# Moving the first scores of a second batch behind the half-steps of an MLP, with later attention work shifted by one to three places

## The chip, the cores and the metric

The kernel runs on one core of a Trainium2 chip. A time is device microseconds (us) of one launch, as the median of three runs. Beside the runs there is one execution taken by the hardware profiler; its span goes from the first to the last instruction of the core.

Five engines work side by side, each through its own queue in order: TensorE (PE: matrix products, with the weight loads shown as PEld), VectorE (DVE), ScalarE (ACT), GpSimd (POOL), and SyncE (SP), which here only issues DMAs. TensorE writes into banks of PSUM, and the other engines read them from there.

## The reference

Windowed attention over 8 batches of 8 heads, 576 tokens, head size 64, and then a two-layer MLP over all 4608 tokens, 512 wide, with 2048 hidden units:

```python
scores = scale * np.matmul(q, k.transpose(0, 1, 3, 2))
mask_plain = (rel >= 0) & (rel < window)                      # window = 32, heads 0-3
mask_dil = (rel >= 0) & (rel < window * dilation) & (rel % dilation == 0)   # dilation = 4, heads 4-7
...
attn = np.exp(scores - max) ; attn = attn / (sum + 1e-09)
x = matmul(attn, v)  ->  (4608, 512)
h = x @ w_in
g = np.where(pos, h, np.where(neg, 0.0, (h + beta) ** 2 / (4.0 * beta)))    # beta = 1
return (g @ w_out).astype(np.float32)
```

The weights are given as 64-bit floats, q and k are 8 times larger than drawn, and the output is 32-bit.

## The kernel before

**The MLP.** The tokens are cut into 9 tiles of 512 (`t`), the hidden units into 16 blocks of 128 (`f`). A *step* `s` is one pair (t, f); there are 144. `layer1(t, f)` makes 12 products of 512 columns into one of two PSUM banks `h` (4 chunks of the model width, three terms each, because a 32-bit factor is split into a high and a low part). Then comes the activation of the step, in this order: `y` on VectorE (L418), a square on ScalarE (L421), `h` on VectorE (L423), a rounded copy `gh` on ScalarE (L424), the remainder `gl` on VectorE (L427). `layer2` makes 12 products into the banks `acc0` to `acc3`, two steps later (`lag = 2`): the loop body of step s is `layer1(s)`, `run(2s)`, `layer2(s-2)`, `run(2s+1)`. The bank `h` of step s is free for step s+2 after its `gl`.

**The slots.** `run(u)` executes what `place(u, ...)` put into slot u. An even slot 2s stands behind `layer1(s)`, an odd slot 2s+1 behind `layer2(s-2)`. So pieces of attention stand between the layers, one piece at a place. In steps 0 and 1 there is no `layer2` yet, so slots 0 and 1, and slots 2 and 3, stand behind the second half of a `layer1`: its first half (chunks 0 and 1) of both steps is issued before the loop.

**The attention.** The heads of batch 0 (0 to 7) are computed before the loop. Those of batch 1 (8 to 15) run in pairs in the slots: `scores_pair(n, 0, 4)` and `scores_pair(n, 4, 6)` are 8 and 4 products (two rows of the trace each), and each product is followed by one VectorE instruction (L182) that adds the mask, writes the scores into `c` and keeps the row minimum (of the negated scores). `after_pair(n)` is the softmax of both heads, and it issues the next load of q and k, on the DMA queue of SyncE. For the heads 8, 9, 10, 12 and 14 `whole(n)` does a subtraction on GpSimd (L297), one exponential on ScalarE (L298) and one sum on VectorE (L299); for the others six exponentials on ScalarE do all three. Then a reciprocal (L291), and a product with it on GpSimd (L292). `transpose_pe(n)` makes six transposes on TensorE into two banks and copies them out (L334: four tiles on ScalarE, two on VectorE). `values_native(n)` is 24 products of the pair (rows L366) into two banks, which `store_x` copies out as `xh` on ScalarE (L350) and `xl` on VectorE (L351). Pairs 10 to 14, all transposes from head 8 on and all values take their banks from the tag `att`, of which there are two, in turn; pair 8's scores alone take `acc0` to `acc3`. Batches 2 to 7 (`scores_split`) follow from slot 27 on, on the same two `att` banks.

**The weights.** `weights(f, ...)` turns a 64-bit block into a high and a low 32-bit part: ScalarE (L116, L122, L132), VectorE (L124, L127) and GpSimd (L133). In steps 1 to 15 the loop prepares block s of `w_out` and s+3 of `w_in`, queued behind the activation of step s-2 (`behind`).

**Who sets the order.** On TensorE and on SyncE's DMA queue the order is that of the program (`manual_schedule`). On the other three engines a planner orders the instructions by when it expects their inputs, and among those that are ready by their place in the program less an offset (`tc.high_priority(offset=...)`): 100 for the row minima and the copies of transposes, 60 for the activation and for `store_x`, none for the weights. Nothing reorders the queues at run time.

**Before the change** pair 8's scores stand before the loop, after the first halves of steps 0 and 1 (L591, L592); `after_pair(8)` is queued behind the last stores of batch 0. At step 2, where TensorE waits for the first activation, 14 products of a constant (`spin(14, acc[0])`, L615) into bank `acc0` stand ahead of `layer1`; they compute nothing that is used.

Of the kernel before, what the change touches and what calls it, by code (L numbers as in the profile page):

```python
# [30 lines left out]
B, H, S, D = 8, 8, 576, 64  # L31
DM, DF = 512, 2048
WIN, DIL = 32, 4
QT, NQ = 96, 6
# [11 lines left out]
def body(ctx, tc, q, k, q2, k2, v, mask, eye, w_in, w_out, out):  # L46
# [105 lines left out]
    def bank(n):  # L152

        if n > H:
            return "att", 2
        turn[0] += 1
        return banks[(turn[0] - 1) % len(banks)]
# [3 lines left out]
    def spin(times, bank):  # L161

        half = half_t.broadcast_to([128, 128])
        for _ in range(times):
            PE.matmul(out=bank[:, :128], lhsT=half, rhs=half, start=True, stop=True)  # L165
# [27 lines left out]
    def scores_pair(n, t0, t1):  # L193

        pair = (n, n + 1)
        plain = n % H < H // 2
        svs = []
        for m in pair:
            if t0 == 0:
                begin(m)  # L200
            tag, bufs = bank(n)
            sp = ps.tile([128, 512], F32, tag=tag, name=f"s{m}_{t0}", bufs=bufs)
            svs.append(sp[:QT, : (t1 - t0) * 128].rearrange("p (t j) -> p t j", j=128))
            if m == 0 and t0 == 0:
                spin(11, sp)
        for t in range(t0, t1):
            for m, sv in zip(pair, svs):
                PE.matmul(
                    out=sv[:, t - t0],
                    lhsT=heads[m]["qs"][:, t * QT : (t + 1) * QT],  # L210
                    rhs=heads[m]["ks"][:, t * QT : t * QT + 128],
                    start=True,
                    stop=True,
                )
        with tc.high_priority(offset=100 if n >= H else 0):
            for t in range(t0, t1):
                for m, sv in zip(pair, svs):
                    which = (0 if t == 0 else 2) if plain else t % 3
                    reduce(m, t, (sv[:, t - t0], msk[:, which]))
# [102 lines left out]
    def pt_of(n):  # L322
        return first_pts[n] if n < len(first_pts) else pts[n % 2]

    def transpose_pe(n):
        pt, c = pt_of(n), heads[n]["c"]
        for t0, t1 in ((0, 4), (4, NQ)):
            tag, bufs = ("att", 2) if n == 0 or n >= H else bank(n)
            tp = ps.tile([128, 512], F32, tag=tag, name=f"t{n}_{t0}", bufs=bufs)
            for t in range(t0, t1):  # L330
                PE.transpose(tp[:, QT * (t - t0) : QT * (t - t0 + 1)], c[:, t], ident)  # L331
            copy = nc.scalar.copy if t0 == 0 else nc.vector.tensor_copy
            with tc.high_priority(offset=100):
                copy(out=pt[:, t0:t1], in_=tp[:, : QT * (t1 - t0)].rearrange("p (t j) -> p t j", j=QT))  # L334
# [62 lines left out]
    def layer1(t, f, cs=range(NC), bank=("h", 2)):  # L397
        xh, xl = xtile(t)
        if cs[0] == 0 and (t, f) not in hps:
            hps[t, f] = ps.tile([128, TOK], F32, tag=bank[0], name=f"h{t}_{f}", bufs=bank[1])  # L400
        hp = hps[t, f]
        terms = [(w, x, c) for c in cs for w, x in ((0, xh), (1, xh), (0, xl))]
        for i, (w, x, c) in enumerate(terms):
            PE.matmul(  # L404
                out=hp,
                lhsT=wi[f][:, w, 128 * c : 128 * c + 128],
                rhs=x[:, c],
                start=c == 0 and i == 0,
                stop=c == NC - 1 and i == len(terms) - 1,
            )  # L410
        if cs[-1] < NC - 1:
            return
        del hps[t, f]
        y = pool.tile([128, TOK], F32, tag="y", name=f"y{t}_{f}")
        gh = pool.tile([128, TOK], F32R, tag="gh", name=f"gh{t}_{f}", bufs=2)
        gl = pool.tile([128, TOK], F32R, tag="gl", name=f"gl{t}_{f}", bufs=2)
        with tc.high_priority(offset=60):
            nc.vector.tensor_scalar(  # L418
                out=y, in0=hp, scalar1=-1.0, scalar2=1.0, op0=ALU.max, op1=ALU.min
            )  # L420
            nc.scalar.activation(out=y, in_=y, func=AF.Square, bias=half_t, scale=0.5)  # L421

            activated = nc.vector.tensor_tensor(out=hp, in0=hp, in1=y, op=ALU.max)  # L423
            copied = nc.scalar.copy(out=gh, in_=hp)  # L424
            if t == 0:
                last["g", f] = copied, activated
            nc.vector.tensor_tensor(out=gl, in0=hp, in1=gh.bitcast(F32), op=ALU.subtract)  # L427
        gs[t, f] = gh, gl

    acc = {}  # L430
# [28 lines left out]
    def place(u, *ops):  # L459
        slots.setdefault(u, []).extend(ops)  # L460

    def after_pair(n):
        softmax(n)
        softmax(n + 1)
        if n + 4 < native:
            load_pair(n + 4)
        elif n + 4 == native:
            load(native)
        else:
            split(native)  # L470
            load(native + 1)
# [8 lines left out]
    def values_native(n):  # L480
        values(n)
        if n + 2 < native:
            load_values(n + 2)

    for n, at in ((8, (5, 6, 7)), (10, (1, 2, 8, 9, 10)), (12, (11, 12, 16, 17, 18)), (14, (19, 20, 24, 25, 26))):
        if n > H:
            place(at[0], lambda n=n: scores_pair(n, 0, 4))
            place(at[1], lambda n=n: (scores_pair(n, 4, NQ), after_pair(n)))
        place(at[-3], lambda n=n: transpose_pe(n))
        place(at[-2], lambda n=n: transpose_pe(n + 1))  # L490
        place(at[-1], lambda n=n: values_native(n))
    for n in range(native, nhead, 2):
        u = 27 + 4 * (n - native)
# [47 lines left out]
    def early_values(n):  # L541
        with tc.high_priority(offset=150):
            values(n)
# [14 lines left out]
    with tc.manual_schedule(engines={mybir.EngineType.PE, mybir.EngineType.SP}):  # L558
        pair(0)
        pair(2)  # L560
        pair(4)
        pair(6)
        hps[0, 0] = ps.tile([128, TOK], F32, tag="h", name="h0_0", bufs=2)
        early_transposes(0)
        load_values(8)
        fetch(1, w_out, "wo")
        fetch(4, w_in, "wi")
        load_pair(10)
        fetch(2, w_out, "wo")
        fetch(5, w_in, "wi")  # L570
        fetch(3, w_out, "wo")
        for f in range(6, 9):
            fetch(f, w_in, "wi")
            fetch(f - 2, w_out, "wo")
        early_values(0)
        early_transposes(2)
        early_values(2)
        first = marks()
        spin(10, hps[0, 0])
        early_transposes(4)  # L580
        spin(3, hps[0, 0])
        early_transposes(6)
        behind(first, ("wi", 0), ("wi", 1))
        early_values(4)
        second = marks()
        layer1(0, 0, range(2))
        early_values(6)
        third = marks()
        behind(second, ("wi", 2))
        layer1(0, 1, range(2))  # L590
        scores_pair(H, 0, 4)  # L591
        scores_pair(H, 4, NQ)  # L592
        for f in range(9, 14):
            fetch(f, w_in, "wi")
            fetch(f - 2, w_out, "wo")
        with tc.issue_after(third[0].ins), tc.issue_after(third[1].ins):
            after_pair(H)
        behind(third, ("wo", 0), ("wi", 3))
        l2 = 0
        steps = [(t, f) for t in range(NT) for f in range(NF)]  # L600
        lag = 2
        for s in range(len(steps) + lag):
            if s == 3:
                for f, src, name in ((12, w_out, "wo"), (13, w_out, "wo"), (14, w_in, "wi")):
                    fetch(f, src, name)
                for f, src, name in ((14, w_out, "wo"), (15, w_in, "wi"), (15, w_out, "wo")):
                    fetch(f, src, name)
            if 0 < s < NF:
                todo = [("wo", s)]
                if s + 3 < NF:  # L610
                    todo.append(("wi", s + 3))
                behind(last["g", max(s - 2, 0)], *todo)
            if s == 2:
                acc[0] = ps.tile([128, DM], F32, tag="acc0", name="acc0_0")
                spin(14, acc[0])  # L615
            if s < 2:
                layer1(*steps[s], range(2, NC))
            elif s < len(steps):
                layer1(*steps[s])
            run(2 * s)  # L620
            while l2 <= s - lag and l2 < len(steps):
                layer2(*steps[l2])
                l2 += 1
            run(2 * s + 1)
        assert not slots
# [63 lines left out]
```

## Time and profile before

| | us |
|---|---|
| Median of 3 runs (929.95 to 930.34) | 930.11 |
| Span of the profiled execution | 928.6 |
| Time outside the span (difference) | 1.5 |
| TensorE busy in the span | 907.2 |
| VectorE busy | 684.2 |
| ScalarE busy | 487.0 |
| GpSimd busy | 239.6 |

In these views a row is a start, a duration, an engine and a source line, and "out<-in". An idle time in brackets is the time in which the engine stood just before the row, with the instruction whose result it then waited for. TensorE's busy time is that of pipelined products and is no measure of how well it is used; where it stands still is read from the brackets and from the view of waits.

### The profile page before, as it was taken

Reading aid. Unit: us, or ns where it says so; the run is one execution under the profiler, and the core shown is the slowest. Engines: PE = TensorE matmul, PEld = TensorE weight load, DVE = VectorE, ACT = ScalarE, POOL = GpSimd, SP = SyncE. Lnnn points to the kernel's source line nnn. Section 1 sums busy time; section 2 is a strip of 40 time slices with the busy share of each in tenths; the row PEclk is TensorE's granted clock in tenths of the full one; section 3 lists DMA queues with packets and bytes.
Section 4 is the critical chain, followed back from the end, with each engine's and each line's share of the span. In section 5 each row is a group of like instructions: output and inputs, shape, how many; then the busy total and the mean of one; then the engine's idle time right before and its main releaser. Section 6 shows DMA issues by size and latency. Waiting matters only on the chain.

```text
span 928.6 us, 14426 instructions
## 1 busy us (share of the span) xinstructions
PE 907.2 (98%) x4886; PEld 743.4 (80%) x4886; DVE 684.2 (74%) x1982; ACT 487.0 (52%) x1336; POOL 239.6 (26%) x155
## 2 busy tenths in 40 slices
PE   7889989999999999999999999999999999999998
PEld 6667778888888888888888888888888888888886
DVE  6898877878888888878887888888878643334333
ACT  5778865655555555555555555555555322222222
POOL 4566452222222222222222222222222000000000
PEclk9999999999999999999999999999999999999999
DMA  9971001322232223222322123222321010001001
GB/s 351 408 294 54 1 27 46 113 70 70 70 115 69 54 58 102 70 70 70 105 82 68 59 58 115 70 70 71 115 70 43 1 46 1 1 1 46 0 1 46
DMA packets 31018, 73.87 MB, mean 80 GB/s; under 512 B 3520, under 2 KB 3808, under 8 KB 30944
## 3 DMA queue, kind: packets, MB, share of 16 engines
q1 hardware_dynamic: 30944, 72.94, 24.1%
q8 instruction: 39, 0.64, 0.3%
q14 instruction: 35, 0.29, 0.1%
HBM read 63.49 MB, written 9.44 MB: 79 GB/s over the span
## 4 chain that ended last, share of the span: by engine, by line
PE 89%; DVE 5%; ACT 3%; DMA 1%; issue 1%; POOL 1%; DVEq 0%; POOLq 0%; ACTq 0%
PE acc L440 41%; PE h L404 39%; PE s L231 4%; PE o L366 3%; DVE c L182 1%; ACT c L256 1%; DVE wo_raw L124 1%; DMA wi_raw<-w_in 1%; DVE wi_m L127 1%; DVE wo_m L127 1%; PE s L165 1%; PE t L331 0%; POOL c L292 0%; DVE c L299 0%; DVE xl L351 0%
## 5 line engine op out<-in xcount | busy, mean ns | idle before, releaser
L440 PE MATMUL acc<-wo,gh 128*128 128x512 f32 x1152 | 384.0, 395 | 0.0
L404 PE MATMUL h<-xh,wi 128*128 128x512 f32 x1152 | 357.2, 391 | 2.2 <-DVE gl L427 2.2
L440 PEld LDWEIGHTS acc<-wo,gh 128*128 128x128 f32 x1152 | 217.2, 189 | 47.6
L404 PEld LDWEIGHTS h<-xh,wi 128*128 128x128 f32 x1152 | 209.0, 188 | 40.7 <-DVE gl L427 2.6
L440 PE MATMUL acc<-wo,gl 128*128 128x512 f32 x576 | 225.7, 392 | 0.0
L404 PE MATMUL h<-xl,wi 128*128 128x512 f32 x576 | 224.3, 389 | 0.0
L144 POOL TENSOR_TENSOR kk<-kr,kk 128x608 fp32r<-128x608 f32 x48 | 94.8, 1975 | 412.8 <-ACT kk L140 412.8
L256 ACT ACTIVATE c<-c 96x128 f32<-96x128 f32 x330 | 128.9, 391 | 120.6 <-DVE c L182 120.6
L421 ACT ACTIVATE y<-y,consts 128x512 f32<-128x512 f32 x144 | 104.2, 723 | 121.1 <-DVE y L418 121.0
L424 ACT CAST gh<-h 128x512 fp32r<-128x512 f32 x144 | 84.4, 586 | 126.6 <-PE acc L440 124.3
L418 DVE TENSOR_SCALAR y<-h 128x512 f32<-128x512 f32 x144 | 99.2, 689 | 57.7 <-PE h L404 57.4
L423 DVE TENSOR_TENSOR h<-h,y 128x512 f32<-128x512 f32 x144 | 100.6, 699 | 49.7 <-ACT y L421 48.3
L404 PEld LDWEIGHTS h<-xl,wi 128*128 128x128 f32 x576 | 108.2, 188 | 23.1
L427 DVE TENSOR_TENSOR gl<-h,gh 128x512 fp32r<-128x512 f32 x144 | 98.5, 684 | 36.6 <-ACT gh L424 36.6
L440 PEld LDWEIGHTS acc<-wo,gl 128*128 128x128 f32 x576 | 108.6, 189 | 19.8
L307 DVE STREAM_TRANSPOSE pt<-c 32x192 f32<-32x192 f32 x288 | 106.1, 368 | 6.6 <-POOL c L292 3.2
L250 DVE TENSOR_TENSOR c<-s,msk 96x256 f32<-96x256 f32 (+1 forms) x168 | 61.4, 377 | 36.6 <-PE s L231 35.6
L292 POOL TENSOR_TENSOR c<-c 96x768 f32<-96x768 f32 x56 | 82.9, 1482 | 16.4 <-DVE c L291 14.1
L182 DVE CUSTOM_DVE_ANT_0 c<-s,c 96x128 f32<-96x128 f32 x288 | 70.5, 280 | 1.0
L256 ACT ACTIVATION_READ_ACCUMULATOR c<-c 96x1 f32 x330 | 61.8, 187 | 0.0
L350 ACT CAST xh<-o 128x288 fp32r<-128x288 f32 (+8 forms) x112 | 38.5, 383 | 38.9 <-PE o L366 23.8
L231 PEld LDWEIGHTS s<-kk,qs 128*96 128x96 f32 x288 | 46.4, 161 | 15.5
(57 smaller groups left out, 644.9 us busy)
## 6 DMA issues: line engine op xcount, KB each, us to landing
kr<-k_in SPq DMA_DIRECT2D x56, 304.0 KB, 3.4
qr<-q_in SPq DMA_DIRECT2D x56, 288.0 KB, 2.8
vt<-v_in SPq DMA_DIRECT2D x32, 384.0 KB, 4.0
out<-out SPq DMA_DIRECT2D x36, 256.0 KB, 3.1
wi_raw<-w_in SPq DMA_DIRECT2D x16, 512.0 KB, 9.7
wo_raw<-w_in SPq DMA_DIRECT2D x16, 512.0 KB, 9.7
msk<-mask_in SPq DMA_DIRECT2D x1, 144.0 KB, 3.7
ident<-eye_in SPq DMA_DIRECT2D x1, 36.0 KB, 4.4
```

The lines of the kernel that those rows point to most:

```text
L144: nc.gpsimd.tensor_tensor(out=kk[:, 1], in0=hd["kr"], in1=kk[:, 0].bitcast(F32), op=ALU.subtract)
L231: PE.matmul(out=sv[:, t - t0], lhsT=hd["qs"][:, t * QT : (t + 1) * QT], rhs=hd["ks"][:, :, t * QT : t * QT + 128], start=True, stop=True,)
L256: last["act"] = nc.scalar.activation(out=c[:, t], in_=c[:, t], func=AF.Exp, bias=st[:, 0, t : t + 1], scale=-1.0, accum_out=st[:, 1, t : t ...
L292: nc.gpsimd.tensor_tensor(out=c, in0=c, in1=spread(st[:, 2]), op=ALU.mult)
L307: nc.vector.transpose(out=pt[r : r + 32, :, 32 * g : 32 * g + 32], in_=c[32 * g : 32 * g + 32, :, r : r + 32],)
L404: PE.matmul(out=hp, lhsT=wi[f][:, w, 128 * c : 128 * c + 128], rhs=x[:, c], start=c == 0 and i == 0, stop=c == NC - 1 and i == len(terms) - 1,
L418: nc.vector.tensor_scalar(out=y, in0=hp, scalar1=-1.0, scalar2=1.0, op0=ALU.max, op1=ALU.min)
L421: nc.scalar.activation(out=y, in_=y, func=AF.Square, bias=half_t, scale=0.5)
L423: activated = nc.vector.tensor_tensor(out=hp, in0=hp, in1=y, op=ALU.max)
L424: copied = nc.scalar.copy(out=gh, in_=hp)
L427: nc.vector.tensor_tensor(out=gl, in0=hp, in1=gh.bitcast(F32), op=ALU.subtract)
L440: PE.matmul(out=acc[m], lhsT=g[:, r], rhs=wo[f][:, w], start=f == 0 and i == 0, stop=f == NF - 1 and i == len(terms) - 1,)
```

## The change

Four things change. Pair 8's scores go into slots 1 and 3, behind the second halves of steps 0 and 1, and lose the rule that queued their softmax behind the stores of batch 0. All later places of batch 1 move: pair 10's scores from slots 1, 2 to 4, 5; its transposes from 8, 9 to 10, 11; its values from 10 to 12; pair 12 by one place; pair 14's scores by one, its transposes from 24, 25 to 25, 26 with head 15 ahead of head 14, its values from 26 to 29. Pair 8's transposes move from 5, 6 to 7, 8, its values from 7 to 9. The activation gets an offset of 120, and so precedes the row minima and all other work with a priority, in every step. `spin(14)` becomes `spin(6)`.

```diff
-        with tc.high_priority(offset=60):
+        with tc.high_priority(offset=120):
             nc.vector.tensor_scalar(
                 out=y, in0=hp, scalar1=-1.0, scalar2=1.0, op0=ALU.max, op1=ALU.min
             )
...
-    for n, at in ((8, (5, 6, 7)), (10, (1, 2, 8, 9, 10)), (12, (11, 12, 16, 17, 18)), (14, (19, 20, 24, 25, 26))):
-        if n > H:
-            place(at[0], lambda n=n: scores_pair(n, 0, 4))
-            place(at[1], lambda n=n: (scores_pair(n, 4, NQ), after_pair(n)))
-        place(at[-3], lambda n=n: transpose_pe(n))
-        place(at[-2], lambda n=n: transpose_pe(n + 1))
+    for n, at in ((8, (1, 3, 7, 8, 9)), (10, (4, 5, 10, 11, 12)), (12, (12, 13, 17, 18, 19)), (14, (20, 21, 25, 26, 29))):
+        place(at[0], lambda n=n: scores_pair(n, 0, 4))
+        place(at[1], lambda n=n: (scores_pair(n, 4, NQ), after_pair(n)))
+        turns = (n, n + 1) if n < 14 else (n + 1, n)
+        for u, m in zip(at[-3:-1], turns):
+            place(u, lambda m=m: transpose_pe(m))
         place(at[-1], lambda n=n: values_native(n))
...
-        scores_pair(H, 0, 4)
-        scores_pair(H, 4, NQ)
         for f in range(9, 14):
             fetch(f, w_in, "wi")
             fetch(f - 2, w_out, "wo")
-        with tc.issue_after(third[0].ins), tc.issue_after(third[1].ins):
-            after_pair(H)
         behind(third, ("wo", 0), ("wi", 3))
...
-                spin(14, acc[0])
+                spin(6, acc[0])
```

After the change slot 12 holds two pieces, the values of pair 10 and then the first scores of pair 12, and slot 29 the values of pair 14 and then the last scores of head 16.

## The prediction

> **What bounds the kernel now.** I read the page first, then the waits, then TensorE's timeline around the change. The page's forty slices show the engine that sets the end, and the one behind it:
>
> ```profile
> PE   7889989999999999999999999999999999999998
> DVE  6898877878888888878887888888878643334333
> ```
>
> TensorE is full from the fourth slice on. Every microsecond in which it stands still early is therefore paid at the end one for one, if nothing later has slack to take it up. The waits of TensorE, over the whole span, say how much there is:
>
> ```profile
> PE s L208 <- DVE c L182: 3.8, 7, 1.2
> PE t L331 <- POOL c L292: 2.8, 2, 2.6
> PE h L404 <- DVE gl L427: 2.2, 2, 1.2
> PE o L366 <- DVE pt L334: 1.8, 1, 1.8
> PE t L331 <- DVE xl L351: 1.4, 1, 1.4
> ```
>
> No wait is listed for the steady part (batches 2 to 7). All that the change can win or lose lies before about 150 us, in these holes:
>
> ```profile
> 38.22 1.55 PE L208 MATMUL s<-kr,qr 64*96 64x128 f32 x24
> 39.70 0.73 PE L404 MATMUL h<-xh,wi 128*128 128x512 f32 x2
> ...
> 41.27 1.12 PE L208 MATMUL s<-kr,qr 64*96 64x128 f32 x16
> 42.32 0.74 PE L404 MATMUL h<-xh,wi 128*128 128x512 f32 x2
> ...
> 45.18 0.46 PE L208 MATMUL s<-kr,qr 64*96 64x128 f32 x2 [1.19 <-DVE c L182]
> 46.03 0.67 PE L208 MATMUL s<-kr,qr 64*96 64x128 f32 x6 [0.39 <-DVE c L182]
> 46.63 3.39 PE L165 MATMUL acc<-consts 128*128 128x128 f32 x28
> 51.06 0.73 PE L404 MATMUL h<-xh,wi 128*128 128x512 f32 x2 [1.04 <-DVE gl L427]
> ...
> 58.48 0.73 PE L404 MATMUL h<-xh,wi 128*128 128x512 f32 x2 [1.16 <-DVE gl L427]
> ...
> 66.57 1.37 PE L366 MATMUL o<-pt,vt 128*64 128x96 f32 x24 [1.80 <-DVE pt L334]
> ...
> 72.92 0.36 PE L331 MATMUL t<-ident,c 96*128 96x96 f32 x2 [1.42 <-DVE xl L351]
> ```
>
> From the end of step 1's half to step 2 at 51.06, TensorE does little of use: 1.19 + 0.39 + 1.04 idle and 3.39 of constant products, 6.0 us; step 3 waits 1.16 more. These 7.2 us have one cause, the late first activation:
>
> ```profile
> 38.84 0.85 DVE L124 TENSOR_SCALAR wo_raw<-wo_raw 128x512 uint32<-128x512 uint32 x1
> ...
> 43.61 0.68 DVE L418 TENSOR_SCALAR y<-h 128x512 f32<-128x512 f32 x1
> ...
> 50.33 0.68 DVE L427 TENSOR_TENSOR gl<-h,gh 128x512 fp32r<-128x512 f32 x1
> ```
>
> Step 0's layer1 ends near 41.3, but `gl` only at 51.0: the 24 row minima of both pairs and softmax sums stand ahead of it. VectorE is not idle meanwhile; it is the second bound, as the windows show (columns: PE, PEld, DVE, ACT, POOL busy, then clock):
>
> ```profile
> 44.00:52.00 8.00, 5.39 (x40) 4.71 (x41) 8.00 (x34) 7.53 (x19) 4.05 (x3) 1.00 1.02 405
> 60.00:70.00 10.00, 8.20 (x58) 6.60 (x57) 9.62 (x11) 5.57 (x11) 7.44 (x6) 1.00 0.55 188
> ```
>
> The last large hole is pair 14's first transpose:
>
> ```profile
> 114.37 0.68 PE L208 MATMUL s<-kr,qr 64*96 64x128 f32 x8
> ...
> 128.71 0.71 PE L331 MATMUL t<-ident,c 96*128 96x96 f32 x6 [2.56 <-POOL c L292]
> ```
> ```profile
> 129.43 4.37 PE acc L440 x12
> ...
> 141.44 2.73 PE h L404 x12
> ```
> ```profile
> 126.00:136.00 10.00, 7.44 (x33) 5.96 (x33) 6.66 (x12) 4.37 (x9) 3.48 (x3) 0.83 0.01 2
> ```
>
> (The last rows are of the chain of waits and of the windows.) The hole costs twice: 2.56 idle, and after it a layer takes 4.37 where others take 2.73 (1.64 more): the granted clock of these ten microseconds is 0.83, against 1.00 in the windows above.
>
> **The change part by part.**
>
> *Start (steps 0 to 3).* The products moved are the same, 24 rows here and 24 there, so their TensorE time cancels. After the change TensorE goes at 38.22 straight into step 0's half (39.70 to 41.27 before: 1.57), 8 products of pair 8 (41.27 to 42.32: 1.05), step 1's half (about 1.57) and 4 products (0.68): 43.1. Then the 6 constant products wait for bank `acc0`, the bank of head 8's last two tiles, so for the third-last of pair 8's row minima. VectorE's work from 38.84 on is then: two weight blocks (to 41.16), 12 minima (2.54, two rows each), and y, h and gl of step 0 and y of step 1 (0.68 each: 2.7):
>
> ```profile
> 41.16 2.54 DVE c L182 x24
> ```
>
> That ends at 46.4 if all of it lies ahead of that minimum. Six constant products take 6/14 of 3.39: 1.45. So step 2's layer1 starts at about 47.9, and from 43.1 the hole is 4.8 where it was 7.2: **+2.4**. Pair 10's scores now come after step 2 and step 0's layer2 and have a layer between their halves; their wait of 1.19 + 0.39 is inside the 7.2. Best case: only one `y` ahead of that minimum, and `gl` in time (44.4 and 1.45: step 2 at 45.9, hole 2.8), +4.4. Worst: `gl` ends where it ends now, at 51.0, hole 7.9, -0.7.
>
> *Steps 3 to 5: 1.80 at pair 8's values and 1.42 at head 10's transposes.* Both are VectorE running late: the copy `pt` and the store `xl` sit in an in-order queue behind weight work that stretches to several times its length whenever GpSimd runs:
>
> ```profile
> 53.41 2.82 DVE L124 TENSOR_SCALAR wo_raw<-wo_raw 128x512 uint32<-128x512 uint32 x1
> ...
> 68.73 0.41 DVE L124 TENSOR_SCALAR wo_raw<-wo_raw 128x512 uint32<-128x512 uint32 x1
> ```
>
> The change removes no VectorE work, and keeps the distances (values one layer after head 9's transposes, head 10's transposes one layer after the values). I let the 1.42 stand and take half of the 1.80: **+0.9**. Ends: both go, +3.2; or a VectorE that is full to the brim gives back the whole lead of the start, -2.9.
>
> *Pair 14.* The chain from the end of its last scores (115.05) to head 14's normalised `c` (just before 128.71) is 13.6 us. Four layers of 2.73 cover 10.9 now. After the change the distance from slot 21 to slot 26 is five layers and head 15's transposes (0.5): 14.15. Head 15 goes first; its `c` is ready by 122.9, almost six us earlier:
>
> ```profile
> 121.44 1.47 POOL L292 TENSOR_TENSOR c<-c 96x768 f32<-96x768 f32 x1 [1.37 <-DVE c L291]
> ```
>
>  The cover is 0.5, and a `y` ahead of the minima (0.68) can eat it, so I leave a hole of 0.4: **+3.8** of 4.2. Ends: +4.2, and +2.4 (a hole of 1.80, which at 66.57 did not lower the clock). Pair 12 moves as a whole by one place: nothing.
>
> *Two slots with two pieces.* New waits arise in slots 12 and 29. Values take both `att` banks, and the scores right behind them need those banks again, after `store_x` has emptied them. Now a layer lies between:
>
> ```profile
> 79.28 1.21 PE L366 MATMUL o<-pt,vt 128*64 128x96 f32 x24
> ...
> 83.41 1.12 PE L208 MATMUL s<-kr,qr 64*96 64x128 f32 x16
> ```
> ```profile
> 72.48 0.29 DVE L351 TENSOR_TENSOR xl<-o,xh 128x128 fp32r<-128x128 f32 x1
> ...
> 82.88 0.28 DVE L351 TENSOR_TENSOR xl<-o,xh 128x128 fp32r<-128x128 f32 x1
> ```
> ```profile
> 137.00 1.21 PE L366 MATMUL o<-pt,vt 128*64 128x96 f32 x24
> ```
> ```profile
> 139.81 0.72 DVE L351 TENSOR_TENSOR xl<-o,xh 128x224 fp32r<-128x224 f32 x2
> ```
>
> Pair 10's values end at 80.5, their last `xl` at 83.16: 2.7 us, hidden so far by layer2. Queued behind the waiting scores is everything else on TensorE: layer2(4) and all that follows. At slot 12 I take 2.5 (floor 1.2, the last two stores alone). At slot 29 one bank is needed; its second piece is the first of the two `xl` at 139.81, done about 1.9 after the values; there the weight work is nearly over, so 1.2 (floor 0.9). Together **-3.7**; best -2.1.
>
> *What costs nothing.* The priority in the steady part: minima come later by at most 3 x 0.69, and a bank of `scores_split` is needed again two layers (5.4 us) later; without that cover each delay would be a hole in each of 48 heads. The removed queueing of pair 8's softmax: its inputs now come later than those stores. SyncE's queue: pair 14's q and k, and the weight loads behind them, now issue after pair 10's scores, some 8 us later, and two of them after the transposes of heads 8 and 9. These blocks are needed from step 11 on, beyond 100 us. The v of pair 10 is next in the queue; it issues after head 9's transposes, four layers (10.9 us) ahead of its use, and takes 4.0:
>
> ```profile
> vt<-v_in SPq DMA_DIRECT2D x32, 384.0 KB, 4.0
> ```
>
> Sum: 2.4 + 0.9 + 3.8 - 3.7 = 3.4 us. The profiled span of 928.6 becomes 925.2; with the 1.5 us by which the median of 930.11 exceeds it, **926.7**.
>
> **The rivals.**
>
> *VectorE gives the lead back.* TensorE arrives earlier, but the same minima, sums and weights must pass VectorE, all busy from 44 to 52 and 96% from 60 to 70; the holes at 66 and 73 grow by what the start won. Then start and steps 3 to 5 sum to 0, and 3.8 - 3.7 leaves 930.0. For it: the windows. Against: from 84 to 100 us VectorE is as full (15.87 of 16) and TensorE hardly waits.
>
> ```profile
> 84.00:100.00 16.00, 15.75 (x85) 12.40 (x81) 15.87 (x42) 13.71 (x33) 9.48 (x7) 1.00 0.20 65
> ```
>
> *Slower: the doubled slots drain slowly and the clock falls.* Pair 8's values end at 67.9 and their last `xl` at 72.8, 4.8 us later, because VectorE was behind; the new priority puts the activation ahead of the stores. If slot 12 drains so, and slot 29 in 1.9, and each is followed by a slow layer (1.64), the slots cost 4.8 + 1.9 + 3.3 = 10.0 and the sum is -2.9: 933.0. It decides once a hole reaches the 2.56 that was followed by slow products; the 1.80 was not.
> [...]
>
> *All of it arrives:* 4.4 + 3.2 + 4.2 - 2.1 = 9.7, so 920.4. It asks for an unhindered VectorE, against the windows.
>
> *The change doesn't do what it says.* The planner places what is ready, so `gl` may still come after minima; the start and the hole at 66.57 then win nothing, and the time is again 930.0.
>
> **How the numbers follow.** Forecast (922 to 928.2): 0.50. All of it: 0.12. VectorE gives it back: 0.20. No effect on the order: 0.04. Slower: 0.14. So faster by over 0.2% 0.62, within 0.2% (1.9 us, about what a measurement can tell from no change) 0.24, slower 0.14. The range runs from 921.5, just short of the best case, to 933.0, the slow one; the unfavourable ends are not all taken together.
>
> **What would show it.** Right: step 2's layer1 starts at 46 to 48.5 us with `gl` already done, and the constant products wait for a row minimum; no hole above 1 us ahead of heads 14 and 15, and a clock of 1.00 between 120 and 140 us; a new wait of scores for `xl` in slots 12 and 29, together 2 to 5 us; no hole after 160 us. Wrong: step 2 still at 50; holes at pair 8's values or head 10's transposes above 2 us; a granted clock below 0.95 near slots 12 or 29; any wait of TensorE in batches 2 to 7, which would mean that the priority costs something in every step.

## The result, and the profile after

The changed kernel takes 937.75 us (936.01 to 938.49, 4 runs) against 930.06 before: a ratio of 1.0081, with a 95% interval of 1.0069 to 1.0094. It is slower by 7.7 us where 3.4 us of gain were forecast, and 4.75 us above the upper end of the range. The profiled execution has a span of 936.0 us.

The page's slices of the changed kernel, engines and then the granted clock in tenths:

```profile
PE   7789999999999999999999999999999999999998
DVE  6886687888888888878888888888888643334333
PEclk9979999999999999999999999999999999999999
```

The steady part is as full as before; the third slice (47 to 70 us) has TensorE at 8 and a clock of 7, and VectorE there is *less* busy than before. The waits of TensorE:

```profile
PE s L208 <- DVE c L182: 7.4, 8, 4.1
PE acc L165 <- DVE c L182: 3.5, 1, 3.5
PE s L208 <- DVE xl L351: 2.8, 3, 1.7
PE s L231 <- DVE xl L351: 1.5, 1, 1.5
PE t L331 <- ACT pt L334: 1.1, 1, 1.1
```

The waits for `gl`, for GpSimd's `c`, of values for `pt` and of transposes for `xl` are gone. In their place stand waits of scores for row minima (L182) and for stores of values (`xl`). In TensorE's timeline they are:

```profile
41.81 0.68 PE L208 MATMUL s<-kr,qr 64*96 64x128 f32 x8
45.95 2.12 PE L165 MATMUL acc<-consts 128*128 128x128 f32 x12 [3.46 <-DVE c L182]
51.84 1.12 PE L208 MATMUL s<-kr,qr 64*96 64x128 f32 x16
60.02 0.46 PE L208 MATMUL s<-kr,qr 64*96 64x128 f32 x2 [4.12 <-DVE c L182]
60.86 1.16 PE L208 MATMUL s<-kr,qr 64*96 64x128 f32 x6 [0.39 <-DVE c L182]
...
89.39 0.46 PE L208 MATMUL s<-kr,qr 64*96 64x128 f32 x2 [0.50 <-DVE xl L351]
91.52 1.99 PE L208 MATMUL s<-kr,qr 64*96 64x128 f32 x14 [1.68 <-DVE xl L351]
...
115.23 0.39 PE L331 MATMUL t<-ident,c 96*128 96x96 f32 x2 [1.06 <-ACT pt L334]
...
123.19 1.25 PE L208 MATMUL s<-kr,qr 64*96 64x128 f32 x16 [0.65 <-DVE xl L351]
...
154.35 0.45 PE L231 MATMUL s<-kk,qs 128*96 128x256 f32 x2 [1.52 <-DVE xl L351]
```

Slot 5 (60.02) has the largest hole, then the one ahead of the constant products (45.95), slot 12 (89.39, 91.52) and slot 29 (154.35). Three of these are followed by slow products. The windows (columns: PE, PEld, DVE, ACT, POOL busy, then the clock) and two layers in the chain of waits show it:

```profile
46.80:50.20 3.40, 3.40 (x13) 2.92 (x13) 2.94 (x5) 1.33 (x2) 3.40 (x2) 0.51 1.02 403
57.10:60.50 3.40, 0.46 (x2) 0.24 (x2) 3.40 (x16) 1.53 (x3) 2.67 (x3) 1.00 0.00 0
60.50:67.30 6.80, 6.44 (x19) 5.00 (x20) 5.19 (x17) 6.30 (x20) 5.32 (x4) 0.50 0.60 207
87.80:91.20 3.40, 1.55 (x26) 1.14 (x26) 2.51 (x6) 1.87 (x5) 2.43 (x2) 1.00 0.00 0
91.20:98.00 6.80, 6.48 (x25) 5.26 (x26) 1.95 (x17) 1.65 (x8) 0.00 (x0) 0.50 0.01 2
```
```profile
62.03 5.42 PE h L404 x12
...
93.51 5.10 PE acc L440 x12
```

17.0 us run at half clock, in stretches of 3.4, 6.8 and 6.8. The kernel before had one of 3.4:

```profile
126.30:129.70 3.40, 0.98 (x8) 0.94 (x9) 3.40 (x5) 1.56 (x3) 1.90 (x2) 1.00 0.00 0
129.70:133.10 3.40, 3.40 (x9) 2.63 (x9) 1.41 (x4) 1.16 (x3) 1.28 (x1) 0.51 0.00 0
```

**Where the 7.4 us of span come from.** From 38 us on, idle time ahead of TensorE's rows sums to 13.4 us (3.46, 4.12, 0.39, 0.50, 1.68, 1.06, 0.65, 1.52) where it was 9.8 (1.19, 0.39, 1.04, 1.16, 1.80, 1.42, 0.25, 2.56): 3.6 more. The slow layers cost 1.3 at step 2 (4.1 from 47.7 to the scores at 51.84, where it took 2.8), 2.7 at 62.03 and 2.4 at 93.51 (5.42 and 5.10 against 2.73), 6.4 together where it was 1.6: 4.7 more. The constant products take 1.3 less (2.12 for 3.39). That is 7.0. Not in this sum are the scores that run at half clock (1.16 at 60.86 and 1.99 at 91.52; the same rows take 0.67 in e1 and 1.08 in e6, so 1.4 more) and layers ahead of the first scores that began 0.5 us earlier here (36.17 against 36.63): the sum is good to about 1 us. More than half of the loss is clock.

**Why slot 5 waits** is read on VectorE. Pair 10's first scores are done at 53.0; the queue is then at a softmax sum of head 9:

```profile
53.18 0.95 DVE L299 TENSOR_REDUCE c<-c 96x6 f32<-96x768 f32 x1 [0.62 <-ACT c L298]
...
54.15 1.21 DVE L127 SCALAR_TENSOR_TENSOR wi_m<-wi_m,wi_raw 128x512 uint32<-128x512 uint32 x1
55.28 0.68 DVE L418 TENSOR_SCALAR y<-h 128x512 f32<-128x512 f32 x1
55.88 2.57 DVE L127 SCALAR_TENSOR_TENSOR wo_m<-wo_m,wo_raw 128x512 uint32<-128x512 uint32 x1
58.38 0.17 DVE L291 RECIPROCAL c<-c 96x6 f32<-96x6 f32 x1
58.48 0.64 DVE L127 SCALAR_TENSOR_TENSOR wi_m<-wi_m,wi_raw 128x512 uint32<-128x512 uint32 x1
59.05 0.28 DVE L182 CUSTOM_DVE_ANT_0 c<-s,msk 96x128 f32<-96x128 f32 x1
```

The first minimum starts 6.0 us after its scores. Three weight instructions (1.21, 2.57, 0.64: 4.4 us) of blocks that TensorE wants only in later steps stand ahead of it. One of them is stretched to four times its length (2.57 where the next takes 0.64), and VectorE itself waits (0.62) for ScalarE's second exponential. The first one had waited for GpSimd:

```profile
49.49 0.84 ACT L298 ACTIVATE c<-c 96x768 f32<-96x768 f32 x1 [1.91 <-POOL c L297]
```

So VectorE is not simply full: from 44 to 60 us it is busy for 14.20 of 16 us (15.97 before), and stands for 1.8 us ahead of the minima behind ScalarE (0.62, 0.56 and 0.62).

### The profile page after: what moved, and what is told of

Its sections match the earlier page's. It is cut to its first block, busy times and chain, and to the rows that moved or that the text cites. A ratio compares the mean times of both kernels' runs of the same rounds, so it can differ in the third digit from the quotient of the medians.

```text
span 936.0 us, 14400 instructions
## 1 busy us (share of the span) xinstructions
PE 911.1 (97%) x4870; PEld 746.3 (80%) x4870; DVE 678.1 (72%) x1982; ACT 487.0 (52%) x1336; POOL 243.4 (26%) x155
## 4 chain that ended last, share of the span: by engine, by line
PE 91%; ACT 3%; DVE 3%; DMA 1%; POOL 1%; issue 1%; DVEq 0%; POOLq 0%; ACTq 0%
PE acc L440 42%; PE h L404 40%; PE s L231 4%; PE o L366 3%; ACT c L256 1%; DMA wi_raw<-w_in 1%; POOL c L297 1%; PE s L208 1%; DVE c L182 1%; PE s L165 1%; PE t L331 1%; DVE wo_m L127 0%; DVE c L299 0%; ACT wi_raw L122 0%; ACT wi_m L116 0%
## 5 line engine op out<-in xcount | busy, mean ns | idle before, releaser
L418 DVE TENSOR_SCALAR y<-h 128x512 f32<-128x512 f32 x144 | 99.2, 689 | 57.6 <-PE h L404 57.1
L182 DVE CUSTOM_DVE_ANT_0 c<-s,c 96x128 f32<-96x128 f32 x288 | 70.6, 281 | 1.1
L231 PE MATMUL s<-kk,qs 128*96 128x256 f32 x288 | 57.7, 283 | 1.5 <-DVE xl L351 1.5
```

The source lines that it names most:

```text
L231: PE.matmul(out=sv[:, t - t0], lhsT=hd["qs"][:, t * QT : (t + 1) * QT], rhs=hd["ks"][:, :, t * QT : t * QT + 128], start=True, stop=True,)
L418: nc.vector.tensor_scalar(out=y, in0=hp, scalar1=-1.0, scalar2=1.0, op0=ALU.max, op1=ALU.min)
```

## The experiments

All are timed against the kernel before on the same chip.

| run | us | ratio to before, 95% |
|---|---|---|
| as changed | 937.75 | 1.0081 [1.0069, 1.0094] |
| e1, offset 60 | 935.37 | 1.0066 [1.0051, 1.0081] |
| e2, no doubled slots | 930.19 | 1.0005 [0.9995, 1.0014] |
| e3, 14 constant products | 933.97 | 1.0049 [1.0034, 1.0064] |
| e4, before with head 15 first | 927.11 | 0.9974 [0.9965, 0.9984] |
| e5, start as before | 934.17 | 1.0054 [1.0034, 1.0075] |
| e6, constants in another bank | 933.54 | 1.0044 [1.0025, 1.0063] |
| e7, pair 10 a place later, no doubled slots | 927.31 | 0.9977 [0.9967, 0.9986] |
| e8, no doubled slots, offset 60 | 931.17 | 1.0020 [1.0009, 1.0030] |
| e9, weight work left out | 932.58 | 1.0024 [1.0013, 1.0035] |
| e10, before with offset 120 | 929.94 | 1.0002 [0.9992, 1.0011] |
| e11, before with later places | 926.50 | 0.9964 [0.9950, 0.9978] |
| e12, e7 with constants in another bank | 930.14 | 1.0001 [0.9991, 1.0010] |

### The changed kernel with single parts undone

**e1**, the offset back at 60:

```diff
-        with tc.high_priority(offset=120):
+        with tc.high_priority(offset=60):
```

> The changed kernel with the activation's offset back at 60, all else as changed. Theory A (the offset of 120 pushes pair 10's first row minima behind gl of step 1, the weight blocks of step 2 and a reciprocal in VectorE's queue; the 4.12 us hole ahead of pair 10's second scores and the slow layer after it come from that): the minima run by 56 us, the hole at slot 5 falls to under 1.5 us, the layer after it takes 2.7 to 2.8 instead of 5.42, and the time falls by 5 to 7 us, to 931 to 933. Rival B (VectorE is simply full there because pair 8's softmax and pair 10's minima now meet, whatever their order): another wait of 3 us or more takes the hole's place within step 3 or 4, and the time stays within 2 us of 937.7.

TensorE's timeline of e1:

```profile
54.15 0.46 PE L208 MATMUL s<-kr,qr 64*96 64x128 f32 x2 [0.61 <-DVE c L182]
55.59 0.67 PE L208 MATMUL s<-kr,qr 64*96 64x128 f32 x6 [0.98 <-DVE c L182]
...
66.09 0.52 PE L331 MATMUL t<-ident,c 96*128 96x96 f32 x4 [0.86 <-POOL wi L133]
67.94 0.58 PE L331 MATMUL t<-ident,c 96*128 96x96 f32 x2 [1.33 <-DVE pt L334]
...
78.42 0.36 PE L331 MATMUL t<-ident,c 96*128 96x96 f32 x2 [1.11 <-DVE xl L351]
```

The hole at slot 5 falls to 1.6 and the layer after it runs at full clock (56.20 to 59.05), so the order of the queue has a large part in it. But 3.3 us of new waits follow at the transposes of heads 9 and 10, with a half-clock stretch of about 3.4 us from 67.7 on (a granted clock of 0.88 from 60 to 70 us, 0.94 from 70 to 80), and the median falls by only 2.4 us. The executions overlap (934.67 to 937.38 here, 936.01 to 938.49 as changed), so the size of this gain is uncertain. Both theories hold in part.

**e2**, no slot with two pieces:

```diff
-    ((8, (1, 3, 7, 8, 9)), (10, (4, 5, 10, 11, 12)), ..., (14, (20, 21, 25, 26, 29))):
+    ((8, (1, 3, 6, 7, 8)), (10, (4, 5, 9, 10, 11)), ..., (14, (20, 21, 25, 26, 30))):
```

> The changed kernel with no slot that holds two pieces: pair 8's transposes and values one slot earlier (6, 7, 8), pair 10's too (9, 10, 11), so that pair 12's first scores have slot 12 alone; pair 14's values in slot 30 instead of 29. Theory: the holes of 0.50 and 1.68 at slot 12 and the slow layer behind them (5.10 us) go, and the 1.52 at slot 29; 6.0 us in all, so 931 to 933, while the hole at slot 5 stays. Rival: the stores of pair 10's values are late for another reason and the wait moves to the next scores with a slow layer of its own: 936 to 938.

```profile
87.46 1.51 PE L208 MATMUL s<-kr,qr 64*96 64x128 f32 x16
91.84 0.72 PE L208 MATMUL s<-kr,qr 64*96 64x128 f32 x8
```

In this timeline pair 12's scores (87.46, 91.84) wait for nothing, and the hole at slot 5 stays (4.09). The time falls by 7.6 us, 1.6 more than expected. In the changed kernel the scores themselves ran at half clock too (1.99 for 14 rows that take 1.08 in e6; 0.50 from 91.2 to 98.0), which the 6.0 had left out; the other 0.6 or so stays open.

**e3**, 14 constant products again in the changed kernel:

```diff
-                spin(6, acc[0])
+                spin(14, acc[0])
```

> The changed kernel with 14 constant products again in place of 6. Theory A (the clock falls because of the 3.46 us hole ahead of the constant products, and the later slow layers because of holes at slots 5 and 12): eight products more delay step 2 by up to 2 us, the two later slow layers stay, and the time is 0.5 to 2 us longer. Rival C (too few constant products let the clock fall): step 2's layer1 runs at full speed and the time falls by 1 us or more; the layer after slot 5 is faster than 5.42.

```profile
45.60 5.02 PE L165 MATMUL acc<-consts 128*128 128x128 f32 x28 [3.50 <-DVE c L182]
...
59.06 0.46 PE L208 MATMUL s<-kr,qr 64*96 64x128 f32 x2 [1.64 <-DVE c L182]
```

It is 3.8 us faster, so theory A is wrong on the sign, and rival C is right in that step 2's layer is no longer slow. In the timeline of e3 the first half-clock stretch falls on constant products and not on step 2's layer (28 rows take 5.02, where they took 3.39 before; the clock is 0.83 from 40 to 50 us and 0.99 from 50 to 60), and the hole at slot 5 is 2.0 instead of 4.5 (1.64, and 0.39 ahead of the next row), because VectorE's minima run about when they did (from 58.1 instead of 59.05) and TensorE arrives 1.5 us later. The slow layer after slot 5 stays, against rival C (a clock of 0.67 from 60 to 70 us). At slot 12 the half clock lasts one stretch instead of two (0.83 from 90 to 100 us, 0.66 as changed). That last part stays open. The profiled execution (935.38) is the slowest of the four and only 2.5 us faster than the changed kernel's, so the rows do not show all of the 3.8.

**e5**, the start as before, the rest as changed:

```diff
-... (8, (1, 3, 7, 8, 9)), (10, (4, 5, 10, 11, 12)) ...
-        place(at[0], lambda n=n: scores_pair(n, 0, 4))
-        place(at[1], lambda n=n: (scores_pair(n, 4, NQ), after_pair(n)))
+... (8, (1, 3, 7, 8, 9)), (10, (1, 2, 10, 11, 12)) ...
+        if n > H:
+            place(at[0], lambda n=n: scores_pair(n, 0, 4))
+            place(at[1], lambda n=n: (scores_pair(n, 4, NQ), after_pair(n)))
...
+        scores_pair(H, 0, 4)
+        scores_pair(H, 4, NQ)
...
+        with tc.issue_after(third[0].ins), tc.issue_after(third[1].ins):
+            after_pair(H)
```

> The changed kernel with the first part of the change undone: pair 8's scores and softmax before the loop, pair 10's scores in slots 1 and 2 as before; later slots, the offset of 120 and 6 constant products as changed. Theory A (most of the loss is the start: pair 10's scores behind step 2 put 4.1 + 0.4 us of hole and 2.7 us of slow layer into slot 5): no wait at slots 4 and 5 is left to have, the doubled slots 12 and 29 still cost 4 to 6 us, and the time is 931 to 934. Rival C (the missing constant products and the clock decide): step 2's wait returns without cover, its layer is slow, and the time is within 1.5 us of 937.7.

934.17, just above theory A's 931 to 934 and 3.6 below the changed kernel: the start as changed, with its six constant products, costs 3.6 us. (Its four executions spread from 933.13 to 936.96.)

**e6**, the constant products in a free bank:

```diff
-                spin(6, acc[0])
+                spin(12, ps.tile([128, 512], F32, tag="att", name="warm", bufs=2))
```

> The changed kernel with 12 constant products into a bank of the tag att, which nobody uses then, in place of 6 into acc0. They no longer wait for a row minimum of pair 8 and cover the 3.46 us hole ahead of step 2. In VectorE's queue the planner then puts pair 10's first minima ahead of the weight blocks of step 2. Theory A (the hole at slot 5 is the place of the minima in the queue): step 2's layer1 starts at 45 to 46 us and runs at full speed, the hole at slot 5 is under 2 us, and the time falls by 5 to 8 us, to 930 to 933. Rival B (VectorE is full until 60 us, whatever the order): the work that now comes later makes new waits at the transposes of heads 8 and 9, as with the offset of 60, and the time is 934 to 937.

```profile
45.54 0.73 PE L404 MATMUL h<-xh,wi 128*128 128x512 f32 x2 [0.22 <-DVE gl L427]
...
69.18 1.05 PE L366 MATMUL o<-pt,vt 128*64 128x96 f32 x20 [1.44 <-DVE pt L334]
...
75.12 0.52 PE L331 MATMUL t<-ident,c 96*128 96x96 f32 x4 [1.74 <-DVE xl L351]
76.91 0.36 PE L331 MATMUL t<-ident,c 96*128 96x96 f32 x2 [1.27 <-DVE xl L351]
```

In the timeline of e6 step 2 starts at 45.5 at full clock (1.00 from 40 to 50 us) and the hole at slot 5 is 1.3, as theory A has it. Then 4.5 us of waits appear at pair 8's values and head 10's transposes, as rival B has it. The median is 4.2 us below the changed kernel's and lies between the two expectations, but no execution took it: three took 931.45 to 931.97 with a mean granted clock of 0.997 or 0.998, the profiled one among them, and three 935.12 to 935.37 with 0.994. The same program falls into either theory's range, and its slower executions are those with the lower clock.

### Is VectorE's queue badly ordered, or full?

**e9** leaves out two VectorE instructions for three blocks of `w_out`:

```diff
-        else:
+        elif not 1 <= f <= 3:
             nc.vector.tensor_scalar(out=low, ...)
-        nc.vector.scalar_tensor_tensor(out=m, ...)
+        if name == "wi" or not 1 <= f <= 3:
+            nc.vector.scalar_tensor_tensor(out=m, ...)
```

> The changed kernel without the two VectorE instructions (L124, L127) of the blocks 1 to 3 of w_out, so that these blocks lack their shift and their low bits. In the changed kernel these six instructions take 5.5 us of VectorE between 43.5 and 58.5 us, ahead of pair 10's first row minima (59.05). Theory B (VectorE's work up to there sets the hole at slot 5): the minima run by 54 to 55 us, the hole falls from 4.5 to under 1 us, no slow layer follows, and the time is 4 to 7 us shorter, 931 to 934. Rival D (the chain of pair 8's softmax through GpSimd and ScalarE, whose sums stand ahead in VectorE's queue, sets it): VectorE waits instead, the minima stay later than 57 us and the hole above 2.5 us.

The timeline of e9 (its line numbers are one higher), and its windows (POOL is the fifth engine column):

```profile
54.51 0.67 PE L209 MATMUL s<-kr,qr 64*96 64x128 f32 x6 [0.39 <-DVE c L183]
...
67.48 1.20 PE L332 MATMUL t<-ident,c 96*128 96x96 f32 x6 [3.34 <-POOL wi L134]
```
```profile
50.00:60.00 10.00, 9.61 (x55) 7.43 (x52) 9.78 (x32) 8.47 (x22) 10.00 (x8) 1.00 0.64 209
```

With 5.5 us less in the queue the hole at slot 5 is 0.39, TensorE is 96% busy from 50 to 60, and 5.2 us are won. The first minimum of pair 10 starts at 52.7, 6.3 us earlier, while VectorE still stands for 1.8 us behind ScalarE ahead of it (0.46, 1.08 and 0.22): VectorE's load there sets the hole, not those waits. A new wait of 3.3 us then ends with GpSimd, which is busy for all ten microseconds from 50 to 60. That GpSimd is the next bound behind VectorE is likely, but no run tests it.

**e7** and **e12** give TensorE a layer more before pair 10's second scores:

```diff
-... (10, (4, 5, 10, 11, 12)), (12, (12, 13, 17, 18, 19)), (14, (20, 21, 25, 26, 29))
+... (10, (5, 6, 10, 11, 12)), (12, (13, 14, 17, 18, 19)), (14, (20, 21, 25, 26, 30))
...
-        turns = (n, n + 1) if n < 14 else (n + 1, n)
+        turns = (n, n + 1) if n < 12 else (n + 1, n)
```

> The changed kernel with other slots: pair 10's scores one place later (5, 6), pair 12's scores alone in 13 and 14 with head 13 transposed ahead of head 12 (17, 18), pair 14's values alone in 30. The row minima of pair 10 then run when they ran before, near 59 us, but TensorE has a layer more to do meanwhile. Theory A: the hole at slot 5 shrinks from 4.5 to under 2 us and no slow layer follows it; against the run without doubled slots (930.2) this gives 4 to 6 us, so 924.5 to 926.5. Rival B: the hole moves one place and stays above 3 us, 929 to 931.

e12 is e7 with e6's edit to the constant products:

> The run with pair 10's scores one place later and no doubled slots (927.3), with 12 constant products into a bank of the tag att in place of 6 into acc0. Theory B (VectorE full; the hole ahead of pair 10's second scores only takes what the start wins): step 2 starts 2 to 3 us earlier without a slow layer, a hole of the same size comes back within step 3 or 4, and the time is 925.5 to 928. Rival A (order): the start's gain is kept, 922.5 to 925.

Pair 10's second scores, in the timeline of e7 and of e12:

```profile
63.39 1.38 PE L208 MATMUL s<-kr,qr 64*96 64x128 f32 x8 [4.25 <-DVE c L182]
```
```profile
60.88 1.37 PE L208 MATMUL s<-kr,qr 64*96 64x128 f32 x8 [4.77 <-DVE c L182]
```

In e7 the hole moves with the scores and keeps its size, as rival B has it; the time is nevertheless 2.9 us below e2's and lies between the two expectations. Of the 2.9, 1.1 is a wait at the transposes of pair 12 that e2 still has; where the rest comes from isn't resolved. e12 starts step 2 at 46.0 instead of about 48, and the hole is 4.77. At head 10's transposes (78.89 and 80.67) it waits another 1.63 and 1.24, which e7 does not. All of the earlier start is lost, and the time is 2 us above its theory B's expectation (there B is the full VectorE).

**e8** is e2 with the offset at 60:

> The run without doubled slots with the activation's offset at 60 instead of 120. With the doubled slots the offset of 60 gave 2.4 us: the hole at slot 5 shrank from 4.5 to 1.6, and new waits at the transposes of heads 9 and 10 took 3.3. Theory A (order): without the doubled slots the same 2 to 3 us are won, 927 to 928.5. Rival B (VectorE full): pair 8's transposes come a slot earlier here, so the new waits are longer, and the time is 930 to 933.

```profile
72.89 0.55 PE L331 MATMUL t<-ident,c 96*128 96x96 f32 x4 [1.08 <-POOL c L292]
76.75 0.36 PE L331 MATMUL t<-ident,c 96*128 96x96 f32 x2 [3.31 <-DVE xl L351]
```

It is not faster than e2 (931.17 against 930.19): rival B. What slot 5 gains is lost at head 10's transposes.

### The kernel before with single parts done

**e4**, head 15 ahead of head 14 (slots 24 and 25):

```diff
-        place(at[-3], lambda n=n: transpose_pe(n))
-        place(at[-2], lambda n=n: transpose_pe(n + 1))
+        turns = (n, n + 1) if n < 14 else (n + 1, n)
+        for u, m in zip(at[-3:-1], turns):
+            place(u, lambda m=m: transpose_pe(m))
```

> The kernel before with one thing changed: of pair 14, head 15 is transposed first (slot 24) and head 14 second (slot 25). Theory: head 15's product on GpSimd ended at 122.9 us and head 14's at 128.7, so the hole of 2.56 us and the slow layer after it (1.64) go, and the time falls by 3.5 to 4.5 us, to 925.6 to 926.6. Rival: head 14 is still late one layer later, a hole of 1 us or more stays: 927 to 929.

```profile
131.20 0.69 PE L331 MATMUL t<-ident,c 96*128 96x96 f32 x6 [0.94 <-ACT pt L334]
```

2.7 us are won, less than the 3.5 to 4.5 expected. The hole of 2.56 and its slow layer are gone (a clock of 1.00 from 120 to 140 us), so head 14 is no longer late; one of 0.94 is left, for the copy of head 15's transposes on ScalarE. The time lies in the rival's range, by another cause than the rival's.

**e10**, the offset of 120 alone:

> The kernel before with the activation's offset at 120 and nothing else changed: the priority alone. Theory: in the steps after batch 1 it costs nothing, and in the start the first gl is no earlier, because y stands behind pair 8's minima by what the planner expects; some holes move by under 1 us: 929 to 931. Rival: the copies of transposes and stores of values come later and their holes at 66 and 73 us grow: 932 or more.

Nothing: 1.0002, with all holes within 0.1 us of the kernel before. The new priority is free in the steady part, and useless as long as the scores stand where they stood.

**e11**, the start, the offset and the constant products of before, with e4's edit and later places:

```diff
-    ((8, (5, 6, 7)), (10, (1, 2, 8, 9, 10)), (12, (11, 12, 16, 17, 18)), (14, (19, 20, 24, 25, 26))):
+    ((8, (6, 7, 8)), (10, (1, 2, 9, 10, 11)), (12, (12, 13, 17, 18, 19)), (14, (20, 21, 25, 26, 30))):
```

> The kernel before with its own start (pair 8's scores before the loop, pair 10's in slots 1 and 2), its offset of 60 and its 14 constant products, but with later places without doubled slots: pair 8's transposes and values at 6, 7, 8, pair 10's at 9, 10, 11, pair 12 one place later, pair 14 at 20, 21, head 15 transposed at 25, head 14 at 26, values at 30. Theory A (the gain of the change lies in the later places, its loss in the start and the doubled slots): the hole of 2.56 and its slow layer go (4.2), the holes at the values of pair 8 and the transposes of head 10 shrink by 1 to 3 of 3.2: 923 to 925.5. Rival B (VectorE full until 75 us): only pair 14's part is won, as when head 15 went first: 926 to 927.5.

```profile
57.99 0.73 PE L404 MATMUL h<-xh,wi 128*128 128x512 f32 x2 [1.35 <-DVE gl L427]
...
74.58 0.36 PE L331 MATMUL t<-ident,c 96*128 96x96 f32 x2 [2.01 <-DVE xl L351]
```

926.50, the fastest of all, 0.36% below the kernel before and faster than both kernels. It lies in rival B's range: pair 14's hole goes, but those at step 3 (1.35) and at head 10's transposes (2.01) stay. The hole at pair 8's values falls from 1.80 to 0.22, and waits of 1.07 at pair 12's transposes (105.95) and 0.62 at pair 14's first scores (113.88) are new.

**Two by two.** The runs make a table of the start against the doubled slots (the rows of the old start differ from each other in the offset and the constant products as well):

| us | doubled slots | one piece a slot |
|---|---|---|
| start as changed | 937.75 | 930.19 (e2) |
| start as before | 934.17 (e5) | 926.50 (e11) |

The doubled slots cost 7.6 and 7.7, the start 3.6 and 3.7, and the later places win 3.4 (929.88 in that comparison against 926.50). 7.6 + 3.7 - 3.4 = 7.9, where 7.7 were measured. That the rows agree to 0.1 us is in part luck: the executions of e5 alone spread over 3.8 us. The start cannot be parted from the constant products either: with 14 of them the start as changed (e3, 933.97) is as fast as the start as before with six (e5, 934.17). The changed start with 14 and without doubled slots was not run.

## Why the prediction was wrong

- **Start, forecast +2.4, measured -3.6 to -3.7: the step that failed.** Its first half held, the time by luck. Step 2's layer1 starts at 47.7 (forecast 47.9), with `gl` done at 45.5, and the constant products wait for a row minimum. But they start 0.5 us earlier than forecast (45.95 against 46.4), and they take 2.12, at a granted clock of 0.72, where 1.45 was forecast. The sentence that failed is that pair 10's scores "have a layer between their halves; their wait of 1.19 + 0.39 is inside the 7.2". I took the minima to follow their scores; they run 6.0 us later, behind weight work and the softmax of pair 8, which now meets pair 10 in VectorE's queue. About 2 us were won up to step 3 (5.2 us from the last scores to step 2's layer1, and no wait at step 3, where it was 7.2); 4.5 us come back at slot 5, and the clock falls there (0.50 from 60.5 to 67.3). The six constant products were booked as a saving of 1.9 (3.39 less 1.45), with no price for the clock: with 14 of them the same start is 3.8 us faster (e3). I had the windows that show VectorE full, and gave "VectorE gives the lead back" 0.20, but let the holes grow only at the places where they had been.
- **Two slots with two pieces, forecast -3.7, measured -7.6 to -7.7: the term that was mis-sized.** Mechanism and places were right, and the holes nearly so: 2.2 at slot 12 (2.5 forecast) and 1.5 at slot 29 (1.2). What was left out of the sum is the clock, priced at nothing: the layer after slot 12 takes 5.10, and the scores ahead of it run slowly too (0.50 from 91.2 to 98.0). The slower rival had this price (10.0 for both slots) and a decision point of 2.56; the clock fell after 0.50 + 1.68. With the scores' 0.9 and the layer's 2.4 the rows give 7.0; the last 0.6 stays open.
- **The clock.** One slow layer was expected to go and none to come. One went (pair 14), and three came: 6.4 us against 1.6. From 90 to 100 us the granted clock is 0.66, one of the prediction's own signs of being wrong.
- **Pair 14, forecast +3.8:** right in place. Heads 15 and 14 are transposed without a wait; alone (e4) the swap gives 2.7, with a wait of 0.94 for a copy left.
- **Pair 12, forecast 0:** missed. Its transposes wait 1.06 for a copy and the scores behind its values 0.65 for a store (115.23 and 123.19), where 0.25 stood before. Both waits stand in e11 too, which has the old start, so they come with the later places.
- **Steps 3 to 5, forecast +0.9:** no wait is left at pair 8's values or at head 10's transposes, but that is no gain. TensorE had stood still earlier, so VectorE was no longer late. Where TensorE comes earlier (e1, e6, e8) such waits return around the same places, 3.3 to 4.5 us of them.
- **The priority, forecast 0 in the steady part:** right (e10). Within the changed start it is not free: by the medians e1 gives 2.4 us back with doubled slots, while e8 wins nothing without them.
- **SyncE's queue, forecast 0:** no wait of TensorE for a load appears.

## What to carry to other kernels

Where a second engine is nearly full, moving work on the first can move a hole instead of removing it: in e7, e8 and e12 it came back as 3 to 5 us at another place. Less work for the second engine in that stretch (e9) shortened the time by 5.2 us. Two pieces that use the same buffers back to back exposed the drain between them (2.2 us at slot 12, 1.5 at slot 29), so check a list of slots for pairs first. Price every hole with the clock: here 2.2 to 4.5 us idle cost half as much again or more when slow products followed (1.64 after 2.56, 2.7 after 4.12 and 0.39, 2.4 after 0.50 and 1.68). And look at single executions before trusting a median: in e6 three took 931.5 to 932.0 at a mean clock of 0.997 or 0.998, and three 935.1 to 935.4 at 0.994.

## What the runs showed of the hardware

In the kernel before and the changed one the half clock (0.50 or 0.51 granted) comes in stretches of 3.4 or 6.8 us, after a stretch of 3.4 us in which TensorE was busy for 0.5 to 1.6 us (0.98 from 126.3 on before; 0.85 from 43.4 on, 0.46 from 57.1 on and 1.55 from 87.8 on as changed). The busiest such stretch, 87.8 to 91.2, has no single idle time above 1.68: TensorE was busy for 45% of it (1.55 of 3.40), and the clock fell. In the kernel before, holes of 1.80 and 1.42 were not followed by it, and 1.60 busy from 63.2 to 66.6 had a clock of 1.00 behind it. But in e4 the same hole of 1.42 at head 10's transposes (72.18) was: the products are slow from 73.4 to 76.8 (1.06 for two that take 0.63 otherwise; the clock is 0.83 from 70 to 80 us), after a stretch with TensorE busy for 1.89 (70.0 to 73.4), while 1.65 busy from 63.2 to 66.6 had no such effect. So these traces give no threshold, neither of busy time nor of a hole's length, and what decides is not shown.

Where VectorE's weight work met GpSimd's, instructions took longer. The stretched VectorE instructions stood in the prediction (2.82, and 0.41 for the same line later); here the pair of GpSimd subtractions of heads 8 and 9 is slow too, in the timeline of the changed kernel and then of e9, in which three blocks' VectorE work is left out:

```profile
46.06 5.00 POOL L297 TENSOR_TENSOR c<-c 96x768 f32<-96x768 f32 x2 [2.43 <-DVE c L182]
```
```profile
45.44 3.61 POOL L298 TENSOR_TENSOR c<-c 96x768 f32<-96x768 f32 x2 [1.76 <-DVE c L183]
```

The kernel before took 2.9 us for the same two; its GpSimd rows, with those beside VectorE's 2.82 at 53.41:

```profile
43.69 2.90 POOL L297 TENSOR_TENSOR c<-c 96x768 f32<-96x768 f32 x2
...
52.99 1.70 POOL L292 TENSOR_TENSOR c<-c 96x768 f32<-96x768 f32 x1 [2.33 <-DMA kr<-k_in]
54.66 1.29 POOL L133 TENSOR_TENSOR wo<-wo_m,wo 128x512 fp32r<-128x512 f32 x1
```

In the changed kernel three weight instructions of VectorE run from 46.2 to 48.1, each in its usual 0.68, while the first subtraction takes 3.4. So the change did not only reorder: it put pair 8's subtractions beside weight work, and they took 2 us longer, while VectorE waited for what follows from them. Why the two engines' work stretches is not shown. What the rows show is when: VectorE's 2.82 at 53.41 ends at 56.23, 0.3 us after GpSimd's run from 52.99 to 55.95, and in the changed kernel its 2.57 at 55.88 ends at 58.45, 0.5 us after GpSimd's run from 54.77 to 57.91, while `y` (55.28), within that run, keeps its 0.68. The prediction's "whenever GpSimd runs" was too strong: at 46.2 VectorE's three kept their 0.68, and GpSimd's subtraction took 3.4.
